# Converting seven weight pieces in every early step instead of in four steps only, in a fused top-k attention and MLP kernel

## The chip, the cores and the metric

The kernel runs on one core of a Trainium2 chip. The metric is the device time of one execution in microseconds (us). Besides the times of three runs there is one execution that was recorded by the hardware profiler; its instructions, waits and DMAs are what is read here. The core's engines are called PE (matmuls), PEld (PE's weight loads), DVE (vector), ACT (scalar), POOL (general purpose) and SP (its queue issues most DMAs).

## The reference

Two blocks follow each other. Attention has 8 batches, 8 heads, 576 rows and head size 64, and keeps for each row only the 32 largest scores:

```python
scores = scale * np.matmul(q, k.transpose(0, 1, 3, 2))
kth = np.partition(scores, -32, axis=-1)[..., -32:-31]
scores = np.where(scores >= kth, scores, -1e9)
attn = softmax(scores)                 # written out, with 1e-9 in the sum
x = np.matmul(attn, v)                 # -> (4608 tokens, 512)
h = x @ w_in                           # 512 -> 2048
g = np.where(h >= 1, h, np.where(h <= -1, 0, (h + 1) ** 2 / 4))
out = g @ w_out                        # 2048 -> 512
```

The weights `w_in` and `w_out` arrive as 64-bit floats and are computed with as 32-bit floats.

## The kernel before

**Steps.** The work is cut into 144 steps. A step is 128 query rows of two heads: `scores` (PE, line 285, copied by ACT on line 287), the top-32 search (`weights`, DVE, with lines 300 to 386; the two instructions on line 386 end a step's DVE work), the weights brought to the other layout, and `values` (PE, `po` on lines 433 and 441), whose result ACT copies into `xT` (lines 446 and 448). The rounds go in pairs of batches, 36 steps to a pair. Steps overlap: scores of step m+2 are begun in step m, and the values of a step follow one or two steps later.

**Chunks and units.** Four steps (or four half tiles) fill one `xT`, a chunk of 128 tokens; there are 36. When a chunk's last values are done, `mlp` appends its work to the queue `pending`: `hidden(x)` is 8 matmuls of 128x128x128 (`ph`, line 466) followed by the activation on ACT and POOL (lines 470 to 484), and `final(f)` is one 128x512 matmul that counts as four (`py`, line 489). So a chunk has 128 units, and the planner counts in these units. The last eight finals of a chunk are put behind the first hidden parts of the next one.

**The planner.** Nothing is scheduled by the hardware or by a compiler: `manual_schedule` keeps the order in which the Python program issues instructions for PE, DVE, ACT and POOL. A loop over the steps m has seven slots; in each slot it issues a part of the top-k search, perhaps a conversion, transposes, values, scores, keys, and then calls `advance`, which takes units from `pending` at a rate of `EARLY_SHARE` a step in early steps and of `share` in the later ones (what is left, divided by the steps that are left, and never more than is ready). `advance` stops at a unit whose weight pieces are not converted.

**Conversion.** The weights are 64 pieces of 128x256. `load` (line 120) issues on SP the fetch of a piece's raw words; `convert_piece` makes 32-bit floats of them: two activations on ACT (lines 140 and 143), a shift on DVE (line 147, for a quarter of the pieces also line 149), and one or two operations on POOL (lines 151, 153, 160). `convert` (line 537) begins the ACT part one piece ahead. Four pieces are converted before the loop. In steps 0 to 3 all seven slots convert one piece each, after that four of the seven. Raw words of pieces 0 to 27 go to `room`, eight areas in the tiles that will hold the keys and values of batch 1; those pieces are fetched up to seven ahead. Later pieces go to a pool of three buffers and are fetched two or three ahead.

**Early and late.** A step is early while pieces are unconverted at its start. In early steps the attention weights are transposed by PE (`transpose_w`, lines 401 and 407); in late ones POOL scales them (line 339), ACT splits them (`halves`, line 416) and two DMAs transpose them through DRAM (`move_w`). Late steps also read all raw weights a second time, a piece every other step (`inspect`, line 551).

**Keys.** `keys_of(b)` (line 221) is a generator: its first part issues fetches, the next four transpose keys on PE (`pk`, line 240) and copy them with ACT, and one of them fetches the values. For the second and later batches a part is taken in every even step, from the fifth step of the batch before on.

Of the kernel before, what the change touches and what calls it, by code (L numbers as in the profile page):

```python
# [24 lines left out]
def kernel(  # L25
# [75 lines left out]
    n_pieces = NK * DFF // WC + NF * DM // WC  # L101
# [16 lines left out]
    loaded, room = {}, []  # L118

    def load(pool, i, bufs=3):  # L120
        if i < n_pieces and i not in loaded:
            if room and i < 28:
                loaded[i] = room[i % 8]
            else:
                loaded[i] = pool.tile([P, 2 * WC], U32, name="raw", bufs=bufs)
            nc.sync.dma_start(out=loaded[i], in_=pieces_of_weights[i][1].bitcast(U32))
# [45 lines left out]
    def run(ctx, paired):  # L172
# [7 lines left out]
        def whole(x, b):  # L180

            return x[b, :, 0:SM, :].rearrange("h (p c) d -> p h c d", c=NT)
# [24 lines left out]
        def main(i):  # L207
            return slice(0, SM) if i == 0 else slice(TL, S)

        def tail(i):  # L210
            return slice(SM, S) if i == 0 else slice(0, TL)
# [9 lines left out]
        def keys_of(b):  # L221

            kT = stage.tile([P, NHP, S], F32, name="kT")
            k_tl = stage.tile([TL, H, D], F32, name="k_tl", bufs=1)
            got = dict(kT=kT)

            def load_keys(hp):
                k_in = stage.tile([P, NT, 2, D], F32, name="k_in")
                for j in range(2):
                    nc.sync.dma_start(out=k_in[:, :, j, :], in_=whole(k, b)[:, 2 * hp + j])  # L230
                return k_in

            k_in = load_keys(0)
            nc.sync.dma_start(out=k_tl, in_=k[b, :, SM:S, :].rearrange("h p d -> p h d"))
            yield got
            for hp in range(NHP):
                k_next = load_keys(hp + 1) if hp + 1 < NHP else None
                pt = ps.tile([P, NT, P], F32, name="pk", tag="a", bufs=2)
                for c in range(NT):
                    nc.tensor.transpose(pt[:, c, :], k_in[:, c].rearrange("p j d -> p (j d)"), ident)  # L240
                for j in range(2):
                    d = slice(j * D, (j + 1) * D)
                    copy = nc.vector.tensor_copy if b == 0 and hp < 2 and j else nc.scalar.copy
                    copy(kT[d, hp, main(j)], pt[d].rearrange("p c n -> p (c n)"))  # L244
                if hp == 0:
                    pt = ps.tile([P, NHP, TL], F32, name="pkt", tag="a", bufs=2)
                    for h2 in range(NHP):
                        nc.tensor.transpose(pt[:, h2, :], k_tl[:, 2 * h2:2 * h2 + 2].rearrange("p j d -> p (j d)"),
                                            ident[0:TL, 0:TL])
                    for j in range(2):  # L250
                        d = slice(j * D, (j + 1) * D)
                        copy = nc.vector.tensor_copy if b == 0 and j else nc.scalar.copy
                        copy(kT[d, :, tail(j)], pt[d])
                k_in = k_next
                if hp == NHP - 2:
                    got["v"], got["v_tl"] = load_values(b)
                yield got
# [272 lines left out]
        words, late = conversion.enter_context(tc.tile_pool(name="words", bufs=1)), None  # L530
        pending = deque()
        total, spent = len(chunks) * (NK * NF + NF * DM // P), 0
        converted, inspected, due = 0, 0, 0.0

        begun, pipe = 0, deque()

        def convert(time):

            nonlocal converted, begun
            while begun < min(converted + (2 if paired else 1), n_pieces):  # L540
                pipe.append(convert_piece(words, begun, not paired))
                next(pipe[-1])
                begun += 1
            next(pipe.popleft())
            converted += 1
            usable[converted] = time
            for i in range(begun, converted + 6):
                if i < converted + (2 if paired else 3) + (begun > converted) or room and i < 28:
                    load(words, i)

        def inspect():
            nonlocal inspected
            room.clear()
            if paired and inspected < n_pieces:
                inspect_piece(late, inspected)
                inspected += 1


        K_TIME, PIECE_TIME, UNIT_TIME, SLOTS, EARLY_STEPS, EARLY_SHARE = 10.1, 0.55, 0.218, 7, 4, 32
        pe_time, dve_time, done, scored, ready_at, usable = 9.0, 12.0, {}, {}, {}, {0: 0.0}  # L560

        def advance(amount, until):
# [40 lines left out]
        prep = None  # L603
# [43 lines left out]
        next_keys, valued = 1, 0  # L647
# [13 lines left out]
        for m in range(n + 2):  # L661
            early = converted < n_pieces
            if not early and first_late is None:
                first_late = m
            elif not early and late is None:
                conversion.close()
                late = ctx.enter_context(tc.tile_pool(name="late", bufs=1))

            share, left = (total - spent) / (n + 2 - m), sum(x[0] for x in pending)
            for r in sorted(ready):  # L670
                if r + 3 > m and r >= valued:
                    share = min(share, left / (r + 3 - m))
                    left += NK * NF + NF * DM // P
            top_k, parts = None, [0] * SLOTS
            if m < n:
                top_k = weights(state[m], state[m - 1] if m > 0 else None, state[m + 1] if m + 1 < n else None)
                parts = [1] * SLOTS if early else [1, 1, 0, 1, 1, 1, 1]
                start = max(dve_time, scored[m])
                now_converting = range(SLOTS) if m < EARLY_STEPS else range(0, SLOTS, 2)
                dve_time = start + K_TIME + PIECE_TIME * min(len(now_converting), n_pieces - converted)  # L680
                done[m] = dve_time
                state[m]["by_tensor"] = early or m >= n - 2
            for slot in range(SLOTS):
                now = start + (dve_time - start) * (slot + 1) / SLOTS
                for _ in range(parts[slot]):
                    next(top_k, None)
                if m < n and converted < n_pieces:
                    if slot in now_converting:
                        convert(now)
                elif slot == 3 and late is not None:  # L690
                    if m % 2:
                        inspect()
                    elif paired:
                        load(late, inspected, 2)
                if slot == 1 and 1 <= m <= n and state[m - 1]["by_tensor"]:
                    pe_time = max(pe_time, done[m - 1] + 2.0) + 1.0
                    transpose_w(state[m - 1])
                    ready_at[m - 1] = pe_time + 1.8
                if slot == 2 and 1 <= m <= n and not state[m - 1]["by_tensor"]:
                    move_w(state[m - 1])  # L700
                    ready_at[m - 1] = done[m - 1] + 14.0
                if slot == 2 and m == n and paired:
                    judge(ps, att)
                if slot == 2 and (early or m == first_late or m >= n - 1):
                    values_until(m)
                if m == 0 and slot in (1, 2):
                    next(first)
                if slot == 4:
                    begin_at(m + 2)
                    if not early:  # L710
                        values_until(m - 1)
                if slot == (6 if early else 1):
                    queries(m + 3)
                    if m < n and prep is None and next_keys < B and steps[m][0] == next_keys - 1 and steps[m][1] >= 1:
                        prep = keys_of(next_keys)
                    if prep is not None and m % 2 == 0:
                        got = next(prep, None)
                        pe_time += 0.5
                        if got is None:
                            prep, next_keys = None, next_keys + 1  # L720
                        else:
                            keys[next_keys] = got
                advance((EARLY_SHARE if early else share) / SLOTS if m < n else 32.0, now)
            for _ in (top_k if top_k is not None else ()):
                pass
# [50 lines left out]
```

## Time and profile before

| | us |
|---|---|
| median of 3 runs | 1609.65 |
| lowest, highest | 1607.3, 1610.31 |
| profiled execution, its own time | 1610.32 |
| its span, first to last instruction | 1608.5 |
| PE busy | 1514.0 (94% of the span) |
| DVE busy | 1422.1 (88%) |
| ACT busy | 1140.4 (71%) |
| POOL busy | 943.3 (59%) |

The mean granted PE clock of the profiled execution is 0.977 of the full one. In the profile's rows a group is given as line, engine, operation, output<-inputs, shapes and count, then busy us, mean ns of one, and the idle time of the engine just before them with what ended it. A matmul of 32-bit floats leaves two records, so that counts of matmuls are twice those of the code. In the answers on waits the columns are total us, times, longest us. In the table of stretches each row is a window of the span, and each engine has its busy us and its number of instructions in it; PEclk is the granted clock, and the last two columns are DMA.

### The profile page before, as it was taken

The numbers are of one execution on the slowest core, as the hardware profiler recorded it, in microseconds if no ns is written. First come the engines' busy times: TensorE is split into PE (matmuls) and PEld (weight loads), VectorE is DVE, ScalarE is ACT, GpSimd is POOL, SyncE is SP. The second block draws the span as 40 slices with busy tenths as digits, with TensorE's granted clock in tenths as the row PEclk, the third lists the DMA queues.
The fourth block names the chain that finished last, engine by engine and source line by source line (L and its number), as shares of the span: only waits on it lengthen the run. The fifth ranks groups of instructions, "written<-read, shape, count | busy, mean of one in ns | idle before, by whom it ended". The sixth has DMA issues, their size and how long they took to land.

```text
span 1608.5 us, 32395 instructions
## 1 busy us (share of the span) xinstructions
PE 1514.0 (94%) x10925; PEld 1080.7 (67%) x10925; DVE 1422.1 (88%) x4443; ACT 1140.4 (71%) x2308; POOL 943.3 (59%) x1376
## 2 busy tenths in 40 slices
PE   5587999999999999999999999999999999999988
PEld 4465676777667776777667767766666667666665
DVE  7999889999998998999999998999898998889932
ACT  5677567777777767777768877776677776677632
POOL 5766466666555665655556666555555665556640
PEclk7798999999999999999999999999999999999999
DMA  9433246565465556665565545655565555544410
GB/s 252 132 96 110 72 130 174 157 158 153 133 174 161 154 143 173 161 150 145 145 172 159 160 133 157 172 143 140 135 174 146 142 142 130 145 131 126 123 51 16
DMA packets 439056, 227.92 MB, mean 142 GB/s; under 512 B 393056, under 2 KB 401248, under 8 KB 438880
## 3 DMA queue, kind: packets, MB, share of 16 engines
q1 hardware_dynamic: 438880, 225.75, 51.8%
q8 instruction: 88, 1.44, 0.4%
q14 instruction: 88, 0.72, 0.1%
HBM read 62.91 MB, written 86.11 MB: 93 GB/s over the span
## 4 chain that ended last, share of the span: by engine, by line
PE 71%; ACT 13%; POOL 4%; DVE 4%; DMA 4%; issue 3%; SPq 1%; POOLq 0%; ACTq 0%; DVEq 0%
PE ph L466 27%; PE py L489 24%; PE sp L285 8%; PE po L433 7%; ACT halves L416 3%; ACT e L323 3%; DMA wT<-rows 2%; ACT s L287 2%; ACT sign L168 2%; PE pw L401 1%; POOL e L339 1%; POOL r L483 1%; PE po L441 1%; ACT r L470 1%; POOL g L484 1%
## 5 line engine op out<-in xcount | busy, mean ns | idle before, releaser
L466 PEld LDWEIGHTS ph<-xT,w_in 128*128 128x128 f32 x4608 | 554.4, 192 | 118.3 <-issue 79.8
L466 PE MATMUL ph<-xT,w_in 128*128 128x128 f32 x4608 | 576.1, 278 | 14.8 <-ACT xT L446 12.9
L489 PE MATMUL py<-w_out,g 128*128 128x512 f32 x1152 | 558.6, 601 | 7.3 <-ACT y L492 7.1
L482 POOL TENSOR_SCALAR r<-r 128x256 f32<-128x256 f32 x276 | 150.7, 546 | 526.5 <-ACT r L470 526.1
L307 DVE MATCH_REPLACE8 more<-tops,more 128x288 f32<-128x288 f32 x864 | 375.2, 437 | 0.0
L416 ACT COPY halves<-e 128x1152 uint16<-128x1152 uint16 x260 | 288.0, 1153 | 112.7 <-POOL e L339 111.5
L470 ACT ACTIVATE r<-ph,half 128x256 f32<-128x256 f32 (+1 forms) x296 | 139.0, 470 | 241.1 <-PE ph L466 227.9
L489 PEld LDWEIGHTS py<-w_out,g 128*128 128x128 f32 x1152 | 193.5, 191 | 137.0 <-issue 131.2
L386 DVE SCALAR_TENSOR_TENSOR e<-s,kth,e 128x577 f32<-128x577 f32 x288 | 249.2, 900 | 0.1
L484 POOL TENSOR_TENSOR g<-r,g 128x256 f32<-128x256 f32 x280 | 219.6, 784 | 22.0
L323 ACT ACTIVATE e<-s,nmax 128x576 f32<-128x576 f32 x288 | 217.4, 770 | 4.7
L339 POOL TENSOR_SCALAR e<-e,rz 128x576 f32<-128x576 f32 x260 | 218.6, 851 | 0.0
L483 POOL TENSOR_TENSOR r<-r 128x256 f32<-128x256 f32 x276 | 201.5, 730 | 23.0
L300 DVE TENSOR_TENSOR more<-s 128x576 f32<-128x576 f32 x144 | 114.9, 798 | 109.0 <-ACT s L287 108.6
L287 ACT ACTIVATE s<-sp 128x576 f32<-128x576 f32 x288 | 169.2, 638 | 4.5 <-PE sp L285 4.2
L285 PE MATMUL sp<-kT,qT 64*128 64x288 f32 x1024 | 162.0, 433 | 9.9 <-ACT kT L244 9.0
L285 PEld LDWEIGHTS sp<-kT,qT 64*128 64x128 f32 x1024 | 89.6, 188 | 98.9 <-issue 29.1
L433 PE MATMUL po<-wT,v_in 128*64 128x128 f32 x2048 | 145.9, 282 | 10.3 <-DMA wT<-rows 7.9
L433 PEld LDWEIGHTS po<-wT,v_in 128*64 128x64 f32 x2048 | 113.4, 139 | 60.5 <-issue 37.5
L477 ACT ACTIVATE g<-ph,minus 128x256 f32<-128x256 f32 x280 | 131.8, 471 | 0.0
L348 DVE MAX8 tops<-more 128x8 f32<-128x288 f32 x288 | 125.4, 442 | 0.0
L300 DVE TENSOR_TENSOR less<-s 128x576 f32<-128x576 f32 x144 | 117.4, 815 | 0.0
(92 smaller groups left out, 1528.2 us busy)
## 6 DMA issues: line engine op xcount, KB each, us to landing
rows<-halves SPq DMA_DIRECT2D x130, 576.0 KB, 2.8
raw<-in_moe_w_out_dram SPq DMA_DIRECT2D x52, 256.0 KB, 2.8
raw<-in_moe_w_in_dram SPq DMA_DIRECT2D x48, 256.0 KB, 2.9
k_in<-in_k_dram SPq DMA_DIRECT2D x64, 128.0 KB, 3.2
q_in<-in_q_dram SPq DMA_DIRECT2D x32, 256.0 KB, 3.3
v_in<-in_v_dram SPq DMA_DIRECT2D x8, 1024.0 KB, 5.9
out_dram<-y SPq DMA_DIRECT2D x32, 256.0 KB, 3.0
kT<-in_moe_w_in_dram SPq DMA_DIRECT2D x16, 256.0 KB, 4.6
```

Of the source, the lines that this page charges most:

```text
L285: nc.tensor.matmul(o[:, a0 - c0:a1 - c0], qT[d, g, :], kT[d, g, k0:k0 + a1 - a0], start=True, stop=True)
L300: nc.vector.tensor_tensor(out=x, in0=s[:, :, 0:SH], in1=s[:, :, SH:S], op=op)
L307: nc.vector.match_replace(out=st["rest"][:, i, :], in_to_replace=eight(st["tops"], i, r - 8), in_values=src[:, i, :], imm_value=LOWEST)
L323: nc.scalar.activation(e[:, i, :], s[:, i, :], AF.Exp, bias=nmax[:, i:i + 1])
L339: nc.gpsimd.tensor_scalar(st["e"][:, i, :], st["e"][:, i, :], rz[:, i:i + 1], 1.0, ALU.mult, ALU.mult)
L386: nc.vector.scalar_tensor_tensor(out=st["all"][1][:, i, :], in0=st["all"][0][:, i, :], scalar=last[i], in1=st["all"][1][:, i, :], op0=ALU. ...
L416: nc.scalar.copy(halves[:, :, i * S:(i + 1) * S], st["e"][:, i, :].bitcast(U16).rearrange("p (k t) -> p t k", t=2))
L433: nc.tensor.matmul(po[j * D:(j + 1) * D], v_in[:, h, c, :] if c < NT else v_tl[0][:, h, :], wT[:, block(j, c)], start=(c == 0), stop=(c == ...
L466: nc.tensor.matmul(ph[:, i], w_in[:, kk, f * P:(f + 1) * P], xT[:, kk], start=(kk == 0), stop=(kk == NK - 1))
L483: nc.gpsimd.tensor_tensor(out=r, in0=r, in1=r, op=ALU.mult)
L484: nc.gpsimd.tensor_tensor(out=g, in0=r, in1=g, op=ALU.add)
L489: nc.tensor.matmul(py[0], gs[f // group][:, f % group], w_out[:, f, :], start=(f == 0), stop=(f == NF - 1))
```

## The change

Every early step converts in all seven slots until no piece is left. All raw words of the first pass go to the eight areas of `room`, which is kept until the conversion is over (it was cleared by the first `inspect`), and a fetch is issued seven pieces ahead. Since `room` lies in the tiles of batch 1, the keys of batch 1 are begun only when all pieces are converted, and then a part is taken in every step and not in every second one. `EARLY_SHARE` goes from 32 to 48.

```diff
     def load(pool, i, bufs=3):
         if i < n_pieces and i not in loaded:
-            if room and i < 28:
+            if room:
                 loaded[i] = room[i % 8]
...
             converted += 1
             usable[converted] = time
-            for i in range(begun, converted + 6):
-                if i < converted + (2 if paired else 3) + (begun > converted) or room and i < 28:
-                    load(words, i)
+            for i in range(begun, converted + (7 if room else 3)):
+                load(words, i)

         def inspect():
             nonlocal inspected
-            room.clear()
...
-        K_TIME, PIECE_TIME, UNIT_TIME, SLOTS, EARLY_STEPS, EARLY_SHARE = 10.1, 0.55, 0.218, 7, 4, 32
+        K_TIME, PIECE_TIME, UNIT_TIME, SLOTS, EARLY_SHARE = 10.1, 0.55, 0.218, 7, 48
...
             elif not early and late is None:
                 conversion.close()
+                room.clear()
                 late = ctx.enter_context(tc.tile_pool(name="late", bufs=1))
...
-                now_converting = range(SLOTS) if m < EARLY_STEPS else range(0, SLOTS, 2)
+                now_converting = range(SLOTS)
...
                     if m < n and prep is None and next_keys < B and steps[m][0] == next_keys - 1 and steps[m][1] >= 1:
-                        prep = keys_of(next_keys)
-                    if prep is not None and m % 2 == 0:
+                        if next_keys > 1 or converted == n_pieces:
+                            prep = keys_of(next_keys)
+                    if prep is not None and (m % 2 == 0 or next_keys == 1):
                         got = next(prep, None)
```

## The prediction, made before the changed kernel was run

> **What bounds the kernel now.** The slices of the span came first. Three of their rows show two stages:
>
> ```profile
> PE   5587999999999999999999999999999999999988
> DVE  7999889999998998999999998999898998889932
> PEclk7798999999999999999999999999999999999999
> ```
>
> A slice is 40.2 us. In the first four to five PE is busy for half to nine tenths at a clock below full, and DVE is full; from there on PE is full at full clock and DVE has a little air. So it is a DVE stage of some 167 us (steps 0 to 11, while weights are converted) and a PE stage of 130 steps.
>
> Next I cut the span where a step ends, which is at the second of its two DVE instructions on line 386: steps 1-3, 4-11, 12-17, 18-31, then three stretches of exactly 36 steps (32-67, 68-103, 104-139: each has the same mix of tiles, one pair of batches), then the rest.
>
> ```profile
> core 0: us, PE busy (x) PEld busy (x) DVE busy (x) ACT busy (x) POOL busy (x), PEclk, DMA share, GB/s
> 31.00:70.60 39.60, 23.80 (x148) 18.93 (x148) 39.60 (x117) 29.63 (x73) 32.08 (x40) 0.73 0.56 158
> 70.60:167.30 96.70, 74.89 (x540) 59.27 (x540) 89.66 (x284) 67.78 (x167) 59.58 (x82) 0.86 0.34 103
> 167.30:234.50 67.20, 65.65 (x455) 46.10 (x454) 60.09 (x186) 43.80 (x91) 39.42 (x56) 1.00 0.36 100
> 234.50:381.30 146.80, 145.16 (x1113) 103.64 (x1111) 134.86 (x423) 111.93 (x220) 93.79 (x133) 1.00 0.61 160
> 381.30:749.90 368.60, 365.32 (x2690) 260.07 (x2690) 343.21 (x1083) 274.92 (x541) 222.95 (x327) 1.00 0.58 155
> 749.90:1124.10 374.20, 364.66 (x2672) 258.21 (x2668) 343.73 (x1083) 276.73 (x546) 227.24 (x327) 1.00 0.56 153
> 1124.10:1503.90 379.80, 365.70 (x2658) 257.28 (x2658) 344.72 (x1083) 273.59 (x539) 223.94 (x325) 1.00 0.52 141
> 1503.90:1608.50 104.60, 92.69 (x599) 65.86 (x595) 46.87 (x151) 44.25 (x103) 31.87 (x50) 0.97 0.21 55
> ```
>
> The three long stretches decide the case. PE is busy for the same 365 us in each, yet they take 368.6, 374.2 and 379.8 us: PE's idle time grows from 3.3 to 14.1. I asked what PE waited for. In the first stretch no first-layer matmul waits for its tokens at all; in the second and in the third the answers begin or continue with
>
> ```profile
> PE ph L466 <- ACT xT L446: 2.9, 2, 1.6
> ```
>
> ```profile
> PE ph L466 <- ACT xT L446: 9.8, 7, 2.2
> PE ph L466 <- ACT xT L448: 1.9, 1, 1.9
> ```
>
> (total us, times, longest). At a chunk's end PE finishes the last `po`, ACT copies it into `xT`, and the first `ph` of that chunk's MLP reads it. In the order in which PE's instructions stand, that `ph` comes after 11 to 15 us of other matmuls in steps 19 to 55, after 4 to 6 in steps 59 to 87, and directly after the `po` from step 103 on: the planner's backlog (its `pending` units at a chunk's end) shrinks from 128 at step 31 to 68 at step 139. With no backlog, 8 of 9 chunk ends in the last stretch pay 11.7 us together, 1.3 each; the stretch lengths give 1.46 (379.8 less 368.6, plus 8 units fewer at 0.246, over 9).
>
> **The change, part by part.** I followed the planner's arithmetic through both versions. A unit is one 128x128x128 product; its price is PE's busy time over the count, from
>
> ```profile
> L466 PE MATMUL ph<-xT,w_in 128*128 128x128 f32 x4608 | 576.1, 278 | 14.8 <-ACT xT L446 12.9
> L489 PE MATMUL py<-w_out,g 128*128 128x512 f32 x1152 | 558.6, 601 | 7.3 <-ACT y L492 7.1
> ```
>
> Each holds 36 chunks x 64 units = 2304 units: 0.250 and 0.242, mean 0.246 us.
>
> Seven pieces in every step end the conversion in step 8, not 11: late mode begins three steps sooner. Units done by the end of steps 8, 17, 31 and 139: before 64, 312, 768, 4284; after 112, 384, 832, 4288. So 64 units (16 us of PE) move ahead of step 32. But from step 11 on PE is level with what is ready: 32 units a step, 64 or 32 left at chunk ends, and in the built order the first `ph` stands directly behind its `po` at every chunk end from step 11 to step 139, 33 in all, against 10 before. That is the last stretch's state, all the way.
>
> *Steps 0-3*: the same order. 0.
>
> *Steps 4-8.* Before, 70.6 to 133.1, 62.5 us, with 20 pieces and 64 units; after, 32 pieces and 112 units. Floor: seven-piece steps without MLP took 13.2 us (39.6/3, DVE busy throughout) and a four-piece one 10.7 (step 7, 108.4 to 119.1): 4 x 13.2 + 10.7 = 63.5. On top, in three of the four-piece steps with MLP DVE waited for ACT, which was held by `r` behind PE:
>
> ```profile
> DVE units L149 <- ACT units L140: 7.0, 3, 3.1
> ```
>
> 2.3 each; four of the five steps have MLP: 9.2. POOL: 32.08/3 = 10.7 us for seven pieces; step 4 adds four hidden pairs (0.56 + 0.73 + 0.78 us, or 0.42 + 0.78 where ACT squares: some 6.5), 17 us against 13.2, worked off by step 6, which has no MLP. I take 16.0, 15.0, 13.2, 14.0 and 13.8: 72.0, so **+9.5**. Bounds: 63.5 (+1.0, every wait hidden) and 79 (+16.5, POOL's overrun not worked off and PE's half clock, 0.73 in these steps, staying).
>
> A price inside that floor: the DVE shift on line 147 takes longer where POOL converts more, first in steps 1-3, then in steps 4-11:
>
> ```profile
> L147 DVE TENSOR_SCALAR bits<-kT 128x256 uint32<-128x256 uint32 x12 | 5.8, 504 | 0.0
> ```
>
> ```profile
> L147 DVE TENSOR_SCALAR bits<-raw 128x256 uint32<-128x256 uint32 x34 | 12.4, 386 | 0.0
> ```
>
> 0.118 us more for 28 pieces is 3.3 us. The Trainium skill, "SBUF — State Buffer", section "Who interferes with whom", says that DVE and GpSimd hold a shared port pair exclusively, so the later one waits out the whole instruction; that speaks against packing pieces. Were each of the 28 to wait out one POOL add of 0.81 us it would be 22.7 us, an estimate; the two rows show a part of that, and I stay with them.
>
> *Steps 9-17.* The nearest row is the first nine late steps of before (12 to 20, 167.3 to 269.3: 102.0 us, 296 units). After has 272: less 24 x 0.246 = 5.9, plus two bare chunk ends at 1.3: 98.7, against 101.4 for steps 9-17 before: **-2.7**. The transposes on PE of three steps become DMAs in this; the keys of batch 1, now in steps 8 to 12 one after another, put four `pk` there where the row has two, and their fetch has one step (some 10 us) against the 3.2 us that `k_in` takes to land: hidden; were it not, 2 to 3 us once.
>
> *Steps 18-31 and 32-139.* The last stretch had 1168 units, after has 1152 in each 36 steps: 379.8 - 16 x 0.246 = 375.9. Three of these, 1127.7, against 1122.6 before: **+5.1**; steps 18-31 at that pace (14/36) 146.2 against 146.8: **-0.6**. Without the waits, the first stretch gives 368.6 - 24 x 0.246 = 362.7, three of them 1088.1 (-34.5), -2.0 in steps 18-31, -5.3 in 9-17.
>
> *Raw words, seven ahead in the room.* The same 64 fetches; each waits on SP for the reader of the piece eight before, one conversion back. A fetch lands in 2.8 us and is due some 13 us later. 0; the one wait of before (ACT for `raw`, 3.0 us in step 4) may go, which is inside the bounds. The second `v_in` load waits on SP for piece 63, with a query fetch behind it that is wanted steps later. 0.
>
> *Steps 140-143 and the tail*: 72 units left in both. 0.
>
> Sum: 9.5 - 2.7 - 0.6 + 5.1 = +11.3 on the profiled run's 1610.3: 1621.6. The median shown is 0.7 below that run: **1621**.
>
> **The rivals.** *The backlog was worth nothing* (faster). PE is the bound, 64 units leave its stage, and the wait at a chunk's end is made up. With no waits: 9.5 - 5.3 - 2.0 - 34.5 = -32.3, so 1577. It turns on one price: 33 chunk ends x s. At s = 0.98 us the change is worth nothing, below 0.88 it is faster; at half of 1.3 it gives 1599. For it: PE at 99% in the first stretch, and DVE busy only 9.6 of 10.4 us a step. Against: 1.3 and 1.46, by two ways. The Trainium skill's "Perfetto Trace Analysis", section "Optimization Strategy", advises interleaving regimes whose most-contended engine differs, which is what this change does, and so speaks against my forecast; it names no price, and by it the time would be this rival's.
>
> *Evens out*: steps 4-8 at their floor with s at 1.2 to 1.3, or as forecast there with s near 1.05: 1607 to 1613.
>
> *Conversion clogs*: as forecast, but steps 4-8 at 79 us and s at 1.46: 1633. It is the upper end of the forecast's side. That the change does something else than it says is excluded by the built order: pieces end in step 8.
>
> **How the numbers follow.** About 0.2% (3.2 us) can be told from no change. Slower 0.70 (forecast with its upper rival), within 0.2% 0.12, faster 0.18: s is known from 8 waits and a mean of 0.9 is not far off. Range 1603 (s at 0.8) to 1634 (the clogged case); its low end leaves out the unpaid-for backlog.
>
> **What would show it.** Right: step 8 ends near 143 us; `ph` waits for `xT` some 30 times, 35 to 48 us in all; each 36-step stretch takes about 376 us, all alike; ACT's copies `halves` rise from 260 to 266. Wrong: stretches of 363 to 370 us, or a step 8 that ends by 135.

## The result, and the profile after

| | before | changed |
|---|---|---|
| median, us | 1608.47 (4 runs) | 1658.87 (4 runs) |
| lowest to highest | 1607.18 to 1610.31 | 1654.96 to 1662.45 |
| profiled execution, its own time and span | 1610.32, 1608.5 | 1662.45, 1660.6 |

The changed kernel is slower: the ratio is 1.0312, 95% interval 1.0285 to 1.0339. Slower was forecast, at 1621 and at most 1634: the side was right, the size was not.

The slices and the stretches of the changed kernel, cut at the same steps as before (4-8, 9-17, 18-31, three times 36 steps, the rest):

```profile
PE   5678999999999999999999999999999999999998
DVE  7998998999999989999998988999999888999942
PEclk7789999999999999999999999999999999999999
```

```profile
69.50:148.20 78.70, 61.26 (x407) 46.77 (x408) 70.31 (x195) 55.01 (x134) 64.67 (x87) 0.85 0.33 105
148.20:239.40 91.20, 88.04 (x624) 60.83 (x624) 86.23 (x271) 65.48 (x128) 51.72 (x73) 1.00 0.52 137
239.40:392.90 153.50, 144.72 (x1100) 103.33 (x1097) 140.39 (x423) 109.33 (x214) 86.89 (x126) 0.98 0.56 150
392.90:782.40 389.50, 369.52 (x2661) 259.57 (x2658) 358.39 (x1081) 277.87 (x544) 223.29 (x326) 0.98 0.55 147
782.40:1171.80 389.40, 369.60 (x2660) 258.46 (x2658) 356.23 (x1081) 277.77 (x544) 223.45 (x325) 0.98 0.55 147
1171.80:1560.20 388.40, 367.23 (x2642) 257.08 (x2639) 356.12 (x1083) 272.77 (x534) 223.60 (x325) 0.98 0.50 136
1560.20:1660.60 100.40, 89.78 (x579) 63.46 (x575) 47.35 (x150) 43.17 (x99) 29.64 (x48) 0.98 0.21 57
```

The slices look alike, so the loss cannot be read there. The stretches show it: all three 36-step stretches take 388 to 390 us, where before they took 368.6, 374.2 and 379.8. Fewer MLP units are done in them (1152 against 1168 to 1176), yet PE is busy longer (367 to 370 us against 365 to 366), DVE is busy 11 to 15 us longer, and PE's clock is 0.98, not 1.00.

What PE waited for in the middle stretch of the changed kernel:

```profile
PE ph L466 <- ACT xT L446: 14.5, 7, 2.6
PE ph L466 <- ACT xT L448: 1.4, 1, 1.4
```

DVE's three operations that grew in the first stretch (steps 32-67), in the kernel before and then in the changed one:

```profile
L386 DVE SCALAR_TENSOR_TENSOR e<-s,kth,e 128x577 f32<-128x577 f32 x73 | 60.5, 863 | 0.0
L300 DVE TENSOR_TENSOR less<-s 128x576 f32<-128x576 f32 x36 | 29.6, 822 | 0.0
L379 DVE TENSOR_TENSOR_SCAN kth<-tops,seconds 128x25 f32<-128x25 f32 x36 | 10.0, 278 | 0.0
```

```profile
L386 DVE SCALAR_TENSOR_TENSOR e<-s,kth,e 128x577 f32<-128x577 f32 x72 | 67.8, 977 | 0.0
L300 DVE TENSOR_TENSOR less<-s 128x576 f32<-128x576 f32 x36 | 33.6, 933 | 0.0
L379 DVE TENSOR_TENSOR_SCAN kth<-tops,seconds 128x25 f32<-128x25 f32 x36 | 13.7, 380 | 0.0
```

The waits for `xT` are where they were forecast (8 of 9 chunk ends, 15.9 us). The chain that ended last has changed its nature, before and after (shares of the span by engine):

```profile
PE 71%; ACT 13%; POOL 4%; DVE 4%; DMA 4%; issue 3%; SPq 1%; POOLq 0%; ACTq 0%; DVEq 0%
```

```profile
ACT 32%; PE 24%; POOL 19%; DVE 14%; issue 6%; DMA 4%; POOLq 0%; SPq 0%; ACTq 0%; DVEq 0%
```

Most of it is no longer PE's work. A piece of that chain in order of time (start, us, what), one turn of a loop:

```profile
830.22 0.15 ACT xT L446
830.37 0.38 ACT r L470
...
830.84 0.43 POOL r L482
...
831.36 1.00 POOL r L483
...
832.43 0.73 POOL g L484
833.15 0.74 POOL e L339
...
834.98 1.15 ACT halves L416
836.12 0.11 ACT nmax L321
...
836.26 1.44 ACT e L323 x2
837.70 1.07 ACT s L287 x2
838.78 0.16 ACT xT L446
```

From one `xT` copy to the next it is 8.6 us, with work of ACT and POOL alone and the short gaps between. In the trace each of the two works through its instructions in the order in which the program issued them. A hidden part's `r` stands directly behind the `xT` copy on ACT; on POOL the three operations of that hidden part stand ahead of the scaling of the step's weights (`e`); ACT's `halves` waits for that scaling; and behind `halves` on ACT stand the exponentials, the scores that DVE needs next, and the next `xT`.

### The profile page after: what moved, and what is told of

It is laid out like the page before. It is cut to its first block, busy times and chain, and to the rows that moved or that the text cites. A ratio compares the mean times of both kernels' runs of the same rounds, so it can differ in the third digit from the quotient of the medians.

```text
span 1660.6 us, 32277 instructions
## 1 busy us (share of the span) xinstructions
PE 1527.1 (92%) x10865; PEld 1077.2 (65%) x10865; DVE 1474.0 (89%) x4443; ACT 1148.9 (69%) x2299; POOL 947.8 (57%) x1382
## 4 chain that ended last, share of the span: by engine, by line
ACT 32%; PE 24%; POOL 19%; DVE 14%; issue 6%; DMA 4%; POOLq 0%; SPq 0%; ACTq 0%; DVEq 0%
PE ph L466 11%; ACT halves L416 8%; ACT e L323 8%; PE py L489 8%; ACT s L287 6%; POOL e L339 6%; POOL r L483 5%; POOL g L484 5%; ACT sign L168 4%; DVE more L307 3%; POOL r L482 3%; DMA wT<-rows 2%; DVE e L386 2%; ACT r L470 2%; PE po L433 2%
## 5 line engine op out<-in xcount | busy, mean ns | idle before, releaser
L466 PE MATMUL ph<-xT,w_in 128*128 128x128 f32 x4608 | 588.6, 282 | 62.4 <-ACT xT L446 50.7
L482 POOL TENSOR_SCALAR r<-r 128x256 f32<-128x256 f32 x276 | 125.9, 456 | 591.2 <-ACT r L470 591.1
L307 DVE MATCH_REPLACE8 more<-tops,more 128x288 f32<-128x288 f32 x864 | 374.7, 437 | 0.0
L416 ACT COPY halves<-e 128x1152 uint16<-128x1152 uint16 x266 | 296.4, 1152 | 105.4 <-POOL e L339 102.6
L489 PEld LDWEIGHTS py<-w_out,g 128*128 128x128 f32 x1152 | 205.8, 197 | 160.4 <-issue 156.5
L386 DVE SCALAR_TENSOR_TENSOR e<-s,kth,e 128x577 f32<-128x577 f32 x288 | 266.7, 961 | 0.1
L484 POOL TENSOR_TENSOR g<-r,g 128x256 f32<-128x256 f32 x280 | 227.8, 814 | 22.0
L339 POOL TENSOR_SCALAR e<-e,rz 128x576 f32<-128x576 f32 x266 | 234.5, 892 | 0.0
L483 POOL TENSOR_TENSOR r<-r 128x256 f32<-128x256 f32 x276 | 213.1, 772 | 23.0
L300 DVE TENSOR_TENSOR less<-s 128x576 f32<-128x576 f32 x144 | 134.1, 931 | 0.0
```

The lines of the kernel that those rows point to most:

```text
L307: nc.vector.match_replace(out=st["rest"][:, i, :], in_to_replace=eight(st["tops"], i, r - 8), in_values=src[:, i, :], imm_value=LOWEST)
L339: nc.gpsimd.tensor_scalar(st["e"][:, i, :], st["e"][:, i, :], rz[:, i:i + 1], 1.0, ALU.mult, ALU.mult)
L386: nc.vector.scalar_tensor_tensor(out=st["all"][1][:, i, :], in0=st["all"][0][:, i, :], scalar=last[i], in1=st["all"][1][:, i, :], op0=ALU. ...
L416: nc.scalar.copy(halves[:, :, i * S:(i + 1) * S], st["e"][:, i, :].bitcast(U16).rearrange("p (k t) -> p t k", t=2))
L466: nc.tensor.matmul(ph[:, i], w_in[:, kk, f * P:(f + 1) * P], xT[:, kk], start=(kk == 0), stop=(kk == NK - 1))
L483: nc.gpsimd.tensor_tensor(out=r, in0=r, in1=r, op=ALU.mult)
```

## The experiments

Theory A: the loss lies in the late steps and comes from the MLP queue being level with what is ready, whatever the conversion does. (Level: no backlog is kept, so that the first hidden matmul of a chunk stands directly behind the chunk's last values on PE, a bare chunk start.) Rival B: the denser conversion, the room or the later keys cost it. Stretches in the table are steps 32-67, 68-103 and 104-139 of each profiled execution.

| kernel | median, us | ratio to before (95%) | stretches, us |
|---|---|---|---|
| changed | 1658.87 | 1.0312 (1.0285 to 1.0339) | 389.5, 389.4, 388.4 |
| 1 backlog rebuilt | 1602.96 | 0.9972 (0.996 to 0.9983) | 366.6, 377.5, 381.6 |
| 2 before, backlog burnt | 1650.1 | 1.0263 (1.023 to 1.0296) | 379.8, 378.6, 379.7 |
| 3 finals first | 1618.03 | 1.0061 (1.0038 to 1.0084) | 376.0, 380.2, 375.7 |
| 4 four pieces | 1605.69 | 0.9984 (0.9971 to 0.9997) | 367.1, 372.6, 384.2 |
| 5 slots turned | 1683.94 | 1.0488 (1.0453 to 1.0524) | 395.5, 398.4, 390.5 |
| 6 backlog kept | 1576.54 | 0.98 (0.9784 to 0.9816) | 362.2, 362.3, 374.7 |
| 7 rebuilt, finals first | 1592.91 | 0.991 (0.9891 to 0.9928) | 371.5, 371.7, 366.6 |
| 8 no early MLP | 1603.39 | 0.9963 (0.9948 to 0.9978) | 367.4, 369.1, 385.9 |
| 9 hidden parts held | 1595.97 | 0.9927 (0.9903 to 0.9952) | 372.6, 373.4, 367.1 |
| 10 square on ACT | 1622.74 | 1.0085 (1.0064 to 1.0106) | 378.5, 379.5, 377.6 |
| 11 before, backlog kept | 1602.48 | 0.9962 (0.9946 to 0.9978) | 373.1, 371.4, 373.4 |
| 12 the same, slots 0 and 4 | 1587.59 | 0.9851 (0.9819 to 0.9883) | 367.3, 366.8, 373.1 |

**1. Backlog rebuilt** (on the changed kernel)

```diff
+            if not early and m < first_late + 6:
+                share *= 0.5
```

> The changed kernel with one edit: in the first six late steps (9 to 14) the share is halved, so that the planner's backlog at the end of step 31 is 120 units (before: 128, changed: 64) and the first hidden matmul of a chunk again has 4 to 16 us of other matmuls ahead of it until step 83. Theory A (the loss comes from the MLP queue being level with what is ready, whatever the conversion does): steps 32-67 take 367 to 373 us and 68-103 373 to 379, as in the kernel before, not 389; the total is 1608 to 1620. Rival B (the loss comes from the denser conversion, the room or the later keys themselves): the 36-step stretches stay at 385 to 390 us and the total at 1650 to 1660.

Measured: 1602.96, 56 us below the changed kernel with all of its conversion in place, and a little below theory A's range. Its first stretch (the columns are those of the stretches above):

```profile
374.50:741.10 366.60, 365.15 (x2697) 259.97 (x2698) 343.13 (x1081) 275.85 (x547) 223.67 (x327) 1.00 0.57 157
```

DVE is back at 343 us, the clock at 1.00. Rival B falls: the conversion is the changed kernel's, and the late stretches are not.

**2. Before, with its backlog burnt**

```diff
-                pe_time += cost * UNIT_TIME
+                pe_time += cost * (0.15 if converted == n_pieces and spent < 1000 else UNIT_TIME)
...
+            if not early and m < first_late + 16:
+                share *= 1.5
```

> The kernel before, conversion untouched, with its backlog worked off between steps 12 and 31 (share raised by half in 16 late steps, and the planner's unit price lowered until 1000 units are done): 64 units of backlog at the end of step 31, 32 units a step from there on, the first hidden matmul directly behind its values at every chunk end from step 15 on. Theory A: the stretches of 36 steps go from 369, 374 and 380 us to 385 to 390 each, the total to 1635 to 1655. Rival B: the total stays within 5 us of 1608.

Measured: 1650.1, in theory A's range; the old conversion with a level queue is slow too. But the stretches are 379, not 385 to 390. By the planner, 45 of this kernel's 72 hidden parts in a stretch fall in slots 4 and 1 and the rest in 2, 5 and 6; of the changed one 63 fall in slots 5 and 1 and the rest in 6. So being level costs, and it looks as if the place of the work in a step costs again (kernels 9 and 12 test that). The rest of its loss lies in steps 12 to 31, where the backlog is worked off (239.9 us against 214.0, of which 64 more units are 16).

**3. Left-over finals ahead of the new chunk's hidden parts** (on the changed kernel)

```diff
             for x in range(NF // group + LAG):
-                if x < NF // group:
-                    pending.append((NK * group, needed(x * group + group - 1, False), partial(hidden, x), False))
                 if x < LAG:
                     for _ in range(min(GROUP, len(behind))):
                         pending.append(behind.pop(0)[0:3] + (False,))
-                else:
+                if x < NF // group:
+                    pending.append((NK * group, needed(x * group + group - 1, False), partial(hidden, x), False))
+                if x >= LAG:
```

> The changed kernel with one edit: in a new chunk's queue the finals left over from the chunk before stand ahead of the hidden parts and not behind them, so that at each chunk end two finals (1.9 us of PE) lie between the last values and the first hidden matmul; backlog and conversion as in the changed kernel. Theory A1 (the bare chunk start is the whole loss of the late steps): PE's waits of the hidden matmul for xT fall from 50 us to under 10, the stretches go from 389 us to 363 to 370, the total to 1585 to 1600. Theory A2 (hidden parts that fall in the same slots of every chunk, so that ACT and POOL hold each other up, are the larger part): the waits fall, but the stretches only go to 375 to 388 and the total to 1620 to 1655. Rival B: 1655.

Measured: 1618.03, just below A2's range. PE's waits for `xT` fall from 56.4 to 14.7 us in all and the total by 41 us, but the stretches fall only to 376 to 380, not to A1's 363 to 370, and DVE stays at 356 us: the bare chunk start alone is not the loss. The 41 us are not the price of the waits alone either, since by the planner this edit also moved the hidden parts to other slots (27 of 72 to slot 4).

```profile
761.30:1141.50 380.20, 365.00 (x2659) 257.90 (x2658) 356.42 (x1083) 278.42 (x544) 222.45 (x325) 1.00 0.56 151
```

**4. Four pieces a step, the rest of the change kept**

```diff
-                now_converting = range(SLOTS)
+                now_converting = range(SLOTS) if m < 4 else range(0, SLOTS, 2)
```

> The changed kernel with the old pace (four pieces in a step from step 4 on); all raw words still in the room, fetched seven ahead, keys of batch 1 begun after the conversion in step 11 and taken in every step. The planner's backlog is that of the kernel before (128 at step 31). Theory A: 1604 to 1613, the room, the deeper fetch and the late keys cost nothing. Rival B, in the form that the room or the keys cost: over 1620.

Measured: 1605.69. The room for all words, the fetch seven ahead and the keys taken late cost nothing; they gain 0.2%.

**5. Level queue, slots turned from chunk to chunk** (on the changed kernel)

```diff
-                advance((EARLY_SHARE if early else share) / SLOTS if m < n else 32.0, now)
+                part = (2, 0, 1, 2, 0, 1, 1)[(slot + 2 * (m // 4)) % SLOTS] if not early and m < n else 1
+                advance(part * (EARLY_SHARE if early else share) / SLOTS if m < n else 32.0, now)
```

> The changed kernel with the slots' shares of the late steps weighted 2, 0, 1, 2, 0, 1, 1 and the weights turned by two slots from chunk to chunk: the queue stays as level as in the changed kernel (64 units at the end of step 31, the first hidden matmul directly behind its values at every chunk end), but the hidden parts no longer fall in slots 1 and 5 of every step. If the fixed slots are what stretches DVE's operations (356 us of DVE in 36 steps in the three level kernels against 343 in those with a backlog): DVE's busy time falls to 343 to 348 in a stretch and the stretch to 370 to 380, the total to 1615 to 1635. If levelness as such stretches them: DVE stays at 354 to 358, and the total at 1640 to 1660.

Measured: 1683.94, worse than the changed kernel, with DVE still at 354 to 356 us in a stretch. Fixed slots as such are not what stretches DVE; I had the wrong suspect.

**6. Backlog kept at 128 units, 32 units a step** (on the changed kernel)

```diff
+            if not early and m < 124:
+                share = min(share, 16.0 if m < first_late + 6 else 32.0)
```

> The changed kernel with the share at 16 in the first six late steps and at most 32 from there to step 123: a backlog of 128 units stands all the time (14 to 16 us of other matmuls ahead of a chunk's first hidden one), but 32 units a step make the hidden parts fall in slots 0 and 4 of every step from about step 32 on. If fixed slots stretch DVE: 354 to 358 us of DVE in a 36-step stretch and the stretch at 370 to 380, total 1608 to 1640, with hardly any wait for xT. If a backlog is all that counts: DVE at 342 to 346, stretches at 362 to 368 (32 units and no waits), total 1585 to 1600.

Measured: 1576.54, 33 us faster than the kernel before (1609.22 beside it) and the fastest of all, below its expected range.

```profile
71.20:151.50 80.30, 62.82 (x407) 48.65 (x408) 70.81 (x197) 54.85 (x134) 64.63 (x87) 0.83 0.33 101
...
737.20:1099.50 362.30, 359.70 (x2654) 255.28 (x2652) 343.92 (x1081) 276.02 (x544) 236.92 (x325) 1.00 0.59 158
```

Steps 4 to 8 are as dear as in the changed kernel (80.3 us), and this one is the fastest all the same. In the stretch PE does the same 1152 units as the changed kernel's PE in 359.7 us of busy time, not 369.6, with 2.6 us of idle time; 362.3 is what the prediction's rival gave for a stretch without waits (362.7).

**7. Rebuilt backlog and finals first, together**: the edits of 1 and 3.

> The changed kernel with both edits, the halved share in the first six late steps and the left-over finals ahead of a new chunk's hidden parts: cover of 1.9 us at the bare ends of the last stretch, 3 to 14 us before. From the stretches of the two kernels alone (366.6, 377.5, 381.5 us with the reserve; 376 to 380 with the finals first): 365 to 368, 371 to 377, 374 to 380, total 1590 to 1602. If the two do not add up: 1603 or more.

Measured: 1592.91. The total is in its range; the first stretch is 4 us longer than expected and the last one 7 us shorter, so the sum holds better than its parts.

**8. No MLP in the early steps** (on the changed kernel)

```diff
-  ... SLOTS, EARLY_SHARE = 10.1, 0.55, 0.218, 7, 48
+  ... SLOTS, EARLY_SHARE = 10.1, 0.55, 0.218, 7, 0
```

> The changed kernel with an early share of 0: no MLP at all before step 9, so 112 units more are left for the late steps, and the backlog at the end of step 31 is 144 units. It prices what MLP adds to the seven-piece steps: steps 4 to 8 took 78.7 us in the changed kernel, and 63.5 is the floor by the steps without MLP, so 64 to 67 us here if MLP's part on ACT and POOL is the reason; if the pace itself is, 72 or more. Total by the backlog theory 1598 to 1608: the late steps take back the 112 units at 0.246 us each on PE.

Measured: 1603.39, and steps 4 to 8 in

```profile
70.70:137.90 67.20, 36.90 (x244) 29.32 (x244) 65.36 (x195) 46.42 (x112) 53.44 (x67) 0.77 0.40 121
```

The total is in its range and the steps lie just above 64 to 67. So the seven-piece steps themselves are 67.2 us (I had 63.5) and MLP adds 11.5 (I had 8.5).

**9. Hidden parts held back in slots 5 and 6** (on the changed kernel)

```diff
-        def advance(amount, until):
+        def advance(amount, until, held=False):
...
                 cost, pieces, work, _ = pending[0]
+                if held and cost == NK * GROUP:
+                    break
...
-                advance((EARLY_SHARE if early else share) / SLOTS if m < n else 32.0, now)
+                advance((EARLY_SHARE if early else share) / SLOTS if m < n else 32.0, now, not early and m < n and slot > 4)
```

> The changed kernel with hidden parts held back in slots 5 and 6 of the late steps: they are issued in slots 0 and 1 of the next step, behind that step's scaling of the attention weights on POOL. The queue stays level and the first hidden matmul stays directly behind its values on PE at every chunk end. If the loop over ACT and POOL is the cause of the 13 us by which a stretch missed the forecast (ACT's r behind the bare hidden matmul, POOL's r, r and g behind that, POOL's scaling of e behind these, ACT's halves, exponentials and scores behind the scaling): stretches of 365 to 380 us, total 1600 to 1640. If the bare chunk start on PE alone is: 385 us or more, total 1640 to 1660.

Measured: 1595.97, just below the loop theory's range. The queue is level and the chunk start bare on PE, the first `ph` still waits for `xT` at 8 of 9 chunk ends (9.5 us in the middle stretch, 15.9 in the changed kernel), and yet 63 us are gone:

```profile
755.50:1128.90 373.40, 362.48 (x2666) 255.38 (x2662) 346.42 (x1081) 277.08 (x544) 218.72 (x322) 1.00 0.58 154
```

```profile
PE ph L466 <- ACT xT L446: 9.3, 7, 1.8
```

In steps 68 to 83 the traces of the changed kernel and of this one have PE's, ACT's and DVE's work in the same order. POOL's alone differs: once in four steps the scaling stands ahead of a hidden part's three operations and not behind them. These 16 steps took 174.3 us in the changed kernel and take 165.4 here. ACT's `halves`, first of the changed kernel, then of this one, and the chain that ended last, of this one:

```profile
L416 ACT COPY halves<-e 128x1152 uint16<-128x1152 uint16 x266 | 296.4, 1152 | 105.4 <-POOL e L339 102.6
```

```profile
L416 ACT COPY halves<-e 128x1152 uint16<-128x1152 uint16 x266 | 293.2, 1153 | 14.0 <-POOL e L339 13.5
PE 62%; ACT 17%; POOL 8%; DVE 7%; issue 4%; DMA 2%; SPq 0%; POOLq 0%; DVEq 0%; ACTq 0%
```

So the loop, which POOL's order closes, is the cause: with a hidden part's POOL work behind the scaling, `halves` hardly waits for the scaling, and PE's waits shrink with it (27.6 us in all, not 56.4). 8.9 us in 16 steps would be 60 in the 108 steps from 32 to 139, an estimate; there this kernel is 54.2 us shorter than the changed one.

**10. The square on ACT** (on the changed kernel)

```diff
-                if converted < n_pieces and x % 2:
+                if True:
```

> The changed kernel with the square of every hidden part on ACT (0.41 us) and not on POOL (0.78 us); queue and order of PE as in the changed kernel. If the loop over ACT and POOL bounds the level steps, each hidden part on it is shortened by about 0.4 us: with one to two parts in a step 15 to 25 us in a 36-step stretch, 365 to 375 us, total 1600 to 1635. If PE's bare chunk start bounds them, nothing changes: 385 to 390 us a stretch, total 1650 to 1660.

Measured: 1622.74, in the loop theory's range, and 378 to 380 us a stretch: 10 to 11 us less in each, between the two expectations. PE's order is that of the changed kernel. So POOL's part of the loop was on the path, but only some of the saving reached the end.

**11. Before, with its backlog kept**

```diff
+            if not early and m < 124:
+                share = min(share, 32.0)
```

> The kernel before, conversion untouched, with the late share capped at 32 until step 123, so that the backlog it has at step 31 (132 units) is kept and not spent bit by bit. By the backlog theory its stretches become 362, 362 and 375 us as in the kernel with seven pieces and a kept backlog, the total 1582 to 1590; the seven-piece conversion is then worth 5 to 12 us once the backlog is kept. If the gain of that kernel came from the denser conversion, this one stays at 1600 to 1610.

Measured: 1602.48 and 371 to 373 us a stretch. The forecast of 362 is missed, and the total lies where the denser conversion as the source of the gain would put it (1600 to 1610): a backlog alone is not enough. By the planner its hidden parts fall in slots 2 and 6 of every step, those of kernel 6 in slots 0 and 4.

**12. The same, with hidden parts in slots 0 and 4 alone**: the edit of 9 on that kernel, held in all slots but 0 and 4 until step 123.

> The kernel of the run before (old conversion, share capped at 32, backlog kept) with hidden parts issued in slots 0 and 4 of the late steps alone, as they fall by themselves in the kernel with seven pieces and a kept backlog, and not in slots 2 and 6. If the slots explain that 371 to 373 us were measured where 362 were expected: stretches of 361 to 365 us until step 103, total 1578 to 1590; what is then left to the 1576.5 of the other kernel is the worth of the seven-piece conversion. If the old conversion carries the difference itself: the stretches stay at 371 to 373 us and the total at 1600 to 1605.

Measured: 1587.59 in total (expected 1578 to 1590), the stretches at 367 (expected 361 to 365).

```profile
742.40:1109.20 366.80, 361.45 (x2658) 256.80 (x2654) 350.80 (x1083) 275.57 (x545) 233.33 (x325) 1.00 0.59 156
```

Some 15 of the 26 us between kernels 11 and 6 come from the slots. The 11 us left to kernel 6 hardly come from faster conversion: both reach the end of step 31 at 375 us, with 768 (kernel 6) and 752 units done, and 16 units are 4 us of PE. In the profiled executions the difference lies in the stretches (1107.2 against 1099.2 us together), and why 362 and not 367 was not settled.

## Why the prediction was right in its side and wrong in its size

By its own steps, in us of the profiled executions, forecast against measured:

| step of the sum | forecast | measured |
|---|---|---|
| steps 0-3 | 0 | -1.1 |
| steps 4-8 | +9.5 | +16.2 (78.7 against 62.5) |
| steps 9-17 | -2.7 | -10.2 (91.2 against 101.4) |
| steps 18-31 | -0.6 | +6.7 (153.5 against 146.8) |
| steps 32-139 | +5.1 | +44.7 (1167.3 against 1122.6) |
| steps 140-143 and the tail | 0 | -4.2 (100.4 against 104.6) |
| sum | +11.3 | +52.1 |

**The mechanism** named, a level queue, was at work: kernels 1 and 6 give the time back and kernel 2 loses it without the change. It did not decide alone, since kernel 9 is level too and faster than the kernel before. What was to be seen was mostly seen: step 8 ended late (148, with 143 forecast), PE waited for `xT` 30 times and 56.4 us in all (some 30 times and 35 to 48 us forecast), the stretches are alike, `halves` rose to 266. But they are alike at 389 us and not at 376.

**The step that failed** is the price of a level stretch, 375.9 us against 389. I took the last stretch of before for that state. Its chunk starts were bare, but its hidden parts still fell in all slots of two of the four steps of a chunk, and DVE was busy for 344.7 us in it, not 356. So it was not wholly in the state that I priced with it. And I charged the missing backlog as a wait of PE alone. With `xT` awaited ahead of the hidden part, the same lateness went through ACT's and POOL's order into scaling, scores and DVE; the chain of waits of before, with ACT at 13% and POOL at 4%, could not show a loop that was not yet closed. Kernel 9 takes the loop away and leaves a wait at the same chunk ends: 367 to 373 us, 2.5 us or more below my price for a level stretch. Of the 13.5 us by which the middle stretch missed, 5.7 are PE's idle time (19.8 us against 14.1) and 7.8 its busy time (369.6 us against 365.7 less 16 units); some 7 of the latter are PE's half clock, an estimate from the last section, and my sum had put that at nothing in these steps.

**Two terms offset each other.** The seven-piece steps were 6.7 dearer than forecast, for the two reasons of kernel 8 (3.7 and 3.0); steps 9 to 17 were 7.5 cheaper, which no run explains. That they cancel is luck. Steps 18 to 31 missed by 7.3, as a part of the level stretch.

**The rival** "the backlog was worth nothing" is refuted: rebuilding it gives 56 us (kernel 1). Keeping it gives 82 (kernel 6), but with hidden parts in slots 0 and 4, which were worth 15 in kernel 12. The Trainium skill's "Perfetto Trace Analysis", section "Optimization Strategy", advises to interleave regimes. That paid with the backlog kept (kernel 6) or with the hidden parts held back (kernel 9); as the change did it, the PE work moved forward was work that later filled PE's waits.

## What to carry to other kernels

In a hand-made order like this one, queued work that is ready early covers waits; pulling it forward to fill an idle stage can close a loop over engines that work in order later on, so count what is left in the queue at each hand-over before and after, and keep it, or hold it behind what other engines wait for, as kernel 9 does. When a wait is priced, ask what stands behind the waiting instruction on every engine of the way, not on its own alone. And a stretch of the old trace is a price for a new state only if it is wholly in that state: compare the busy time of all engines, not the wait in question.

## What the runs showed of the hardware that I had not expected

PE waits of 1.8 to 2.6 us can halve its clock for the 3.4 us after. Around one chunk end of the changed kernel:

```profile
451.90:455.50 3.60, 3.55 (x35) 2.50 (x34) 3.60 (x12) 3.54 (x7) 0.75 (x2) 1.00 0.51 148
455.50:458.90 3.40, 0.88 (x7) 0.88 (x8) 3.40 (x16) 2.47 (x6) 0.00 (x0) 1.00 0.69 213
458.90:462.30 3.40, 3.40 (x9) 1.85 (x8) 3.40 (x9) 0.84 (x2) 1.78 (x4) 0.50 1.12 316
```

PE idles 2.5 us of the second window and has half its clock in the third. In the changed kernel's steps 32-139 PE waited 1.8 to 2.6 us 22 times, and 12 half-clock stretches of 3.41 us followed (40.9 us together, 4 in each 36-step stretch); the kernel before has one (3.4 us) and kernel 9 none. Half of 40.9 is some 20 us, 7 in each stretch, an estimate for PE's lost time and for the larger part of what its busy time grew by.

The trace also shows why 12 and not 22. The 12 begin at whole multiples of 3.413 us from one another (the first at 458.9 us, the fourth at 762.7, 89 times 3.413 later). In the 3.413 us before each, PE was busy for 0.88 to 1.59 us; in every other stretch of that grid it was busy for 1.55 us or more, and a full clock followed. So here it was not the length of a wait that counted but whether it left PE idle for more than about half of one such stretch. The Trainium skill, "TensorE: Matmul & The Clock Gate", section "HAM oscillation — how this bites in real kernels", asks for no idle gap over some 3.4 us. Here shorter gaps did it.

Two of DVE's operations with two inputs grew by 0.11 us each (863 to 977 and 822 to 933 ns), while a third of that size, `more` on line 300, did not (815 and 808 ns) and POOL did the same work in the same time (223 us in the first stretch). With POOL's work in another place both differ: in the middle stretch of kernel 9 DVE was busy for 346 us and POOL for 219, of kernel 11 for 339 and 209, of kernel 6 for 344 and 237. "SBUF — State Buffer", section "Who interferes with whom", says that the order of issue decides who blocks. That fits, but no run here separates it from other causes, nor says how much of the loss is DVE's growth.
